# Layer 2 of the MLP recut as 448 columns per token block plus 128 turned ones, with the table magnitudes on GpSimd

## The chip, the cores and the metric

The kernel runs on one core of one Trainium2 chip. The metric is the device time of one launch in microseconds (us). An engine is called by its short name in the profile: PE is TensorE's matmul stream, PEld its weight loads, DVE VectorE, ACT ScalarE, POOL GpSimd, SP SyncE; a "q" behind a name is that engine's instruction queue (for DMAs: their issue).

## The reference

Input `u` has 2048 tokens of 576 channels. After a layer norm, two branches are computed and combined. One is a state-space convolution over time, done as an FFT over the tokens; the other is an MLP over the channels:

```python
x  = A_u
xn = layernorm(x)
s  = irfft(rfft(xn^T, 4096) * rfft(K, 4096))[:2048]^T + xn * D_skip   # K[d,t] = 2 Re sum_n C[d,n] exp(A[d,n] dt[d] t), n < 128
h  = gelu(layernorm(xn) @ w1 + b1)                                    # 576 -> 4608
g  = silu(h @ w2 + b2)                                                # 4608 -> 576
return x + s * g
```

All of it is float32. The change touches the second product, `h @ w2 + b2`, its accumulation, the final combination of its rows, and one step in making `K`.

## The kernel before

**The MLP.** Precision comes from splitting: each float32 operand is kept as a high and a low part in TensorE's faster float32 format, and each product is three matmuls (high·high, high·low, low·high). The hidden width 4608 is cut into 12 groups of G = 3 chunks of 128; the 2048 tokens into four blocks of 512, of which two (`tb` 0 and 1) are worked on in the first half of the program and two in the second. A **slot** is one group for one block of 512 tokens. There are 48 slots (numbered 0 to 47). In a slot, layer 1 (`layer1`, line 519) runs 14 matmuls of 512 columns for each of the three chunks. Behind each chunk stands a chain: ACT applies GELU from PSUM (line 552), ACT copies the high part `hh` (555), DVE subtracts for the low part `hl` (558). Layer 2 (`layer2`, line 585) then takes four token blocks `j` of 128: `hh`/`hl` of that block are the stationary operand (128x128) and `w2h`/`w2l` the moving one, in two halves of 288 columns. That makes 4 blocks x 3 chunks x 3 terms x 2 halves = 72 matmuls a slot. DVE adds the sum of each `j` from PSUM into `acc` in SBUF (595). `l2_terms` gives the order: the terms with chunks 0 and 1 of `j` 0 and a piece of `j` 1 come first, so that the chain of the third chunk has time.

**PSUM.** There are eight banks. The tile `cv` holds two pairs of banks for the convolution; `mxa` and `mxb` are one pair each and change roles every slot (`mx`).

**The convolution.** For each of 36 batches of 16 channels (NB), `tables` makes the values from which K is built: `load_par` (810, POOL's queue) fetches the parameters, DVE and ACT compute phases, cosines and sines, `mags` (853) multiplies out two tables of magnitudes `mg` (1024 and 512 elements a partition), and `weigh` (864 to 870) multiplies these with the cosines and sines into `U` and `v`. TensorE then runs `kgen` (910) and the FFT stages (982, 1021, 1074, 1106). This work stands between the MLP's matmuls on every engine.

**The order.** The class `Order` is a planner that runs when the program is built. It keeps a clock for each engine, adds an estimated duration for each step (`dve(n)`, `act(n)`, `pool(n)`, `L1`, `LEN`), and writes the instructions in the order of these clocks; the chip then executes each engine's instructions strictly in that order and the engines wait for each other by semaphores. Steps of the MLP are "urgent" and have due times (`hidden_by`, `add_by`); convolution steps fill in where they do not reach past a due time.

**The end.** The last slot accumulates on top of a seed: ACT copies `acc` into PSUM (`seed`, 567) ahead of the matmuls, ACT then applies SiLU from PSUM (678), DVE multiplies (687) and adds (697), and DMAs store the rows (700). In the slot before it, the rows of the other block are finished from SBUF (682, 689, 693, 697). `gate_store` stores the first half's gates to DRAM, where `combine` fetches them later. `FIRST` are the slots that start a sum (0, 3, 24, 25), `GATE` those that end one in the first half (20 and 23).

Of the kernel before, what the change touches and what calls it, by code (L numbers as in the profile page):

```python
# [38 lines left out]
TB = 512  # L39

# [172 lines left out]
def mixer_kernel(ctx, tc, u, log_a_real, a_imag, c_real, c_imag, log_dt, d_skip, w1, b1, w2, b2,  # L213
# [8 lines left out]
    def bank2(name):  # L222
        return ps.tile([P, 2, TB], F32, name=name, bufs=2 if name == "cv" else 1)
# [100 lines left out]
    acc = sb.tile([P, 8, D], F32, name="acc")  # L324

    def table_memory():

        t = [sb.tile([P, 2, SB, NV], F32, name="w", bufs=2) for _ in range(2)]  # L330
        t = [x.rearrange("p k c t -> p (k c t)") for x in t + [sb.tile([P, 2, SB, 64], F32, name="v")]]
        return [t[k // 3][:, k % 3 * D:(k % 3 + 1) * D] for k in range(8)]

    def x_load(b, queue=nc.sync, two=False):

        if b < 4:
            XT[b] = acc[:, 4 + b]
# [164 lines left out]
    HID, LAST, Q1, Q2 = {}, {}, {}, {}  # L502
    turn = [0]

    def mx(i):
        return "mxa" if (turn[0] + i) % 2 == 0 else "mxb"

    def layer1(g, tb, i):
        h, lo, r1, r2 = W[1]
        c = slice(i * P, (i + 1) * P)  # L510
        if i < 2:
            Q1[i] = bank2(mx(i))
        q = Q1[i % 2][:, i // 2]
# [7 lines left out]

    def first_layer1(i):
# [3 lines left out]
        if i != 1:  # L526
            Q1[i] = bank2("mxb" if i else "mxa")
        q = Q1[2][:, 0] if i == 2 else Q1[0][:, i]
        pairs = [(h, XH, 0), (h, XH, 1), (h, XL, 0), (h, XH, 2), (h, XL, 1), (h, XH, 3), (h, XL, 2), (h, XL, 3)]

        if i != 1:
            for j, (a, b, kb) in enumerate(pairs):
                for k in ((0, 1), (2,))[i // 2]:
                    nc.tensor.matmul(Q1[k // 2 * 2][:, k % 2], a[:, kb, k * P:(k + 1) * P], b[:, kb, 0],  # L534
                                     start=j == 0, stop=False)
        c = slice(i * P, (i + 1) * P)
        for kb in range(KB):
            nc.tensor.matmul(q, lo[:, kb, c], XH[:, kb, 0], start=False, stop=False)
        for r in (r1, r2):
            nc.tensor.matmul(q, r[:, c], XR[:, 0], start=False, stop=r is r2)  # L540

        return [hidden(0, 0, k, Q1[k // 2 * 2][:, k % 2]) for k in ((), (0, 1), (2,))[i]]
# [18 lines left out]
    def seed(tb, j, tile, halves=(0, 1)):  # L561

        d = slice(halves[0], halves[-1] + 1)
        q = bank2(tile)
        for dh in halves:
            SEED[j, dh] = q
        nc.scalar.activation(q[:, d, :288], acc[:, tb * 4 + j].rearrange("p (h d) -> p h d", h=2)[:, d], AF.Copy)

    SEED = {}

    def layer2(g, tb, j, terms, last, alone=False):
# [5 lines left out]
        c = slice(j * P, (j + 1) * P)  # L577
# [1087 lines left out]
```

## Time and profile before

| | |
|---|---|
| time, median of 3 runs | 1073.8 us (1073.32 to 1075.48) |
| the profiled execution's own time | 1074.78 us |
| its span | 1073.0 us |
| granted TensorE clock | 0.999 of full speed |
| first matmul of layer 1 | 12.89 us after the start |
| last matmul starts | 1067.41 us |
| largest group on PE | line 585, 3456 matmuls of 288 columns |
| largest group on DVE | line 558 (`hl`), 144 of 691 ns |
| largest group on POOL | line 810 (DMA issue), 36 of 764 ns |

The profile's page gives busy times of each engine, and the chain of work that ended last, followed back from the last instruction. Matmuls overlap in the pipeline and their ends are modelled, so the spacing of their starts, or the length of a merged piece of the chain divided by its number of matmuls, says more than the mean duration of one.

### The profile page before, as it was taken

The numbers are of one execution on the slowest core, as the hardware profiler recorded it, in microseconds if no ns is written. First come the engines' busy times: TensorE is split into PE (matmuls) and PEld (weight loads), VectorE is DVE, ScalarE is ACT, GpSimd is POOL, SyncE is SP. The second block draws the span as 40 slices with busy tenths as digits, with TensorE's granted clock in tenths as the row PEclk, the third lists the DMA queues.
The fourth block names the chain that finished last, engine by engine and source line by source line (L and its number), as shares of the span: only waits on it lengthen the run. The fifth ranks groups of instructions, "written<-read, shape, count | busy, mean of one in ns | idle before, by whom it ended". The sixth has DMA issues, their size and how long they took to land.

```text
span 1073.0 us, 25798 instructions
## 1 busy us (share of the span) xinstructions
PE 1065.7 (99%) x10703; PEld 926.8 (86%) x10703; DVE 952.1 (89%) x1530; ACT 693.3 (65%) x1063; POOL 206.8 (19%) x294
## 2 busy tenths in 40 slices
PE   9999999999999999999999999999999999999998
PEld 7989999888888888888888888788887888888887
DVE  7789968989898999999999989999999999866657
ACT  6656768867657586686866667667585676525353
POOL 6669433111000001100120000200011022322020
PEclk9999999999999999999999999999999999999999
DMA  7885455654223332356322233232431437454146
GB/s 230 240 257 194 130 194 197 209 116 130 74 66 106 50 90 73 108 142 145 89 73 77 68 75 97 50 99 64 87 97 43 132 100 167 123 185 135 38 117 168
DMA packets 139573, 129.62 MB, mean 121 GB/s; under 512 B 89628, under 2 KB 111296, under 8 KB 138432
## 3 DMA queue, kind: packets, MB, share of 16 engines
q1 hardware_dynamic: 122944, 78.31, 27.3%
q0 software_dynamic: 15760, 48.70, 15.0%
q8 instruction: 84, 1.38, 0.6%
q10 hardware_dynamic: 752, 0.97, 0.3%
q14 instruction: 33, 0.27, 0.1%
HBM read 98.50 MB, written 35.19 MB: 125 GB/s over the span
## 4 chain that ended last, share of the span: by engine, by line
PE 96%; DVE 2%; DMA 0%; ACT 0%; issue 0%; ACTq 0%; DVEq 0%
PE mxa L519 21%; PE mxb L585 21%; PE mxb L519 21%; PE mxa L585 21%; PE cv L910 3%; PE cv L1021 3%; PE cv L982 2%; PE cv L1074 2%; PE cv L1106 1%; DMA acc<-in_A_u_dram 0%; PE cv L585 0%; PE mxa L534 0%; DVE pr L749 0%; DVE row L394 0%; DVE acc L595 0%
## 5 line engine op out<-in xcount | busy, mean ns | idle before, releaser
L585 PE MATMUL mxb<-w2h,hh 128*128 128x288 f32 x573 | 170.2, 297 | 0.0
L585 PE MATMUL mxb<-w2h,hl 128*128 128x288 f32 x573 | 169.6, 296 | 0.0
L585 PE MATMUL mxb<-w2l,hh 128*128 128x288 f32 x573 | 168.6, 294 | 0.0
L585 PE MATMUL mxa<-w2h,hh 128*128 128x288 f32 x567 | 168.5, 297 | 0.0
L585 PE MATMUL mxa<-w2h,hl 128*128 128x288 f32 x567 | 167.9, 296 | 0.2 <-DVE hl L558 0.2
L585 PE MATMUL mxa<-w2l,hh 128*128 128x288 f32 x567 | 166.8, 294 | 0.0
L558 DVE TENSOR_TENSOR hl<-h,hh 128x512 fp32r<-128x512 f32 x144 | 99.3, 691 | 67.8 <-ACT hh L555 67.2
L810 POOL DMA_DIRECT2D par<-par_s x36 | 27.5, 764 | 463.9 <-DVE mg L853 412.2
L552 ACT ACTIVATE h<-mxa,b1t 128x512 f32<-128x512 f32 x73 | 50.1, 688 | 101.7 <-PE mxa L519 97.8
L585 PEld LDWEIGHTS mxb<-w2h,hh 128*128 128x128 f32 x573 | 107.6, 188 | 6.9 <-issue 3.0
L585 PEld LDWEIGHTS mxa<-w2h,hh 128*128 128x128 f32 x567 | 106.5, 188 | 7.4 <-issue 5.3
L585 PEld LDWEIGHTS mxb<-w2l,hh 128*128 128x128 f32 x573 | 107.6, 188 | 0.7
L585 PEld LDWEIGHTS mxb<-w2h,hl 128*128 128x128 f32 x573 | 107.5, 188 | 0.6 <-DVE hl L558 0.3
L585 PEld LDWEIGHTS mxa<-w2h,hl 128*128 128x128 f32 x567 | 106.4, 188 | 0.9 <-DVE hl L558 0.8
L585 PEld LDWEIGHTS mxa<-w2l,hh 128*128 128x128 f32 x567 | 106.5, 188 | 0.7
L552 ACT ACTIVATE h<-mxb,b1t 128x512 f32<-128x512 f32 x71 | 48.9, 689 | 74.8 <-PE mxb L519 71.1
L555 ACT ACTIVATE hh<-h 128x512 fp32r<-128x512 f32 x144 | 90.8, 632 | 4.1
L499 ACT ACTIVATE w2h<-raw 128x576 fp32r<-128x576 f32 x75 | 46.5, 675 | 56.5 <-PE mxa L585 53.5
L519 PE MATMUL mxa<-XH,w1h 128*128 128x512 f32 x284 | 78.7, 399 | 0.0
L519 PE MATMUL mxb<-XH,w1h 128*128 128x512 f32 x280 | 78.1, 401 | 0.0
L519 PE MATMUL mxa<-XL,w1h 128*128 128x512 f32 x284 | 76.2, 390 | 0.0
L519 PE MATMUL mxa<-XH,w1l 128*128 128x512 f32 x284 | 76.0, 389 | 0.0
(251 smaller groups left out, 2497.5 us busy)
## 6 DMA issues: line engine op xcount, KB each, us to landing
raw<-in_B_w_dram SPq DMA_DIRECT2D x75, 288.0 KB, 3.1
raw<-in_B_w_dram SPq DMA_DIRECT2D x100, 192.0 KB, 3.2
par_s<-A POOLq DMA_DIRECT2D x8, 1080.0 KB, 6.0
par<-par_s POOLq DMA_DIRECT2D x36, 240.0 KB, 3.3
f2t<-f2q SPq DMA_DIRECT2D x24, 256.0 KB, 3.3
raw<-in_B_w_dram SPq DMA_DIRECT2D x50, 96.0 KB, 3.6
u_s<-in_A_u_dram POOLq DMA_DIRECT2D x16, 288.0 KB, 4.5
xc<-xn_s SPq DMA_DIRECT2D x48, 96.0 KB, 3.7
```

Source lines behind the costliest of these rows:

```text
L499: nc.scalar.activation(h, r, AF.Copy)
L519: nc.tensor.matmul(q, a, b, start=j == 0, stop=j == len(ops) - 1)
L552: nc.scalar.activation(t, q, AF.Gelu_apprx_tanh, bias=b1t[:, g * G + i:g * G + i + 1], scale=1.0)
L555: LAST[0] = nc.scalar.activation(hh[:, i], t, AF.Copy)
L558: nc.vector.tensor_sub(hl[:, i], t, hh[:, i].bitcast(F32))
L585: nc.tensor.matmul(q[:, dh, :288], a[:, i, c], b[:, i, d], start=i == 0 and k == 0 and not alone, stop=i == G - 1 and k == 2, skip_group_c ...
L810: nc.gpsimd.dma_start(PAR[b].rearrange("p (g i) k -> p g (i k)", g=4), dram(par_s, (b // 6 * CH + b % 6 * 4) * NPAR, [[D * NPAR, P], [24 * ...
L910: nc.tensor.matmul(q[32 * g:32 * g + 32, i // 2, i % 2 * 64:i % 2 * 64 + 64], U[:, ri, 4 * g + i, :], v[:, ri, 4 * g + i, :], start=ri == ...
L982: nc.tensor.matmul(Q1ST[i, x][g // 2][64 * f:64 * f + 64, g % 2].rearrange(order), f1t[r].rearrange("p s k -> p (s k)"), rhs(r, f), start= ...
L1021: nc.tensor.matmul(Q[i][32 * q:32 * q + 32, f, 2 * ri:2 * ri + 2], m[r, 4 * i + q, 32 * ri:32 * ri + 32], A2[r, 4 * p + 2 * i + q // 2, :, ...
L1074: nc.tensor.matmul(QI[q // 2][64 * h:64 * h + 64, q % 2, i], MAT["g2t", p + h][r, i, ri], YS[p + h][0][r, i, ri], start=ri == 0, stop=ri == 1,
L1106: nc.tensor.matmul(Q[f][32 * e:32 * e + 32, t], g1t[r], A2[r, k:k + 2, 1].rearrange("p i d r -> p i r d"), start=True, stop=True, skip_gro ...
```

## The change

It has four parts.

1. **The recut.** Each token block `j` of layer 2 now takes 448 columns in one matmul per chunk and term: 36 matmuls of 448 columns a slot. The other 128 channels of all four token blocks are one piece with the key `"T"`: the stationary operand is `w2`'s 128 columns and the moving one `hh` or `hl` of all 512 tokens, so that the sum stands turned in PSUM (channels on partitions, 512 tokens along the bank): 9 matmuls of 512 columns. In four slots, `TURNED` = 20, 23, 46 and 47, the last ones of each token block, `"T"` is instead computed untransposed, as 36 matmuls of 128 columns. `acc` now holds 4 x 448 columns and 512 turned ones for each `tb`.
2. **Turning back.** Behind the last turned sum of each block (`CONV`: slots 18, 22, 44 and 45) DVE transposes 32x32 blocks into `bias2`, and 16 DMAs on SP put the blocks into place. Behind slot 22 `bias2` is loaded anew.
3. **PSUM and ACT.** `mxa` and `mxb` give way to four single banks `m0` to `m3`. Layer 1 uses banks 0, 1 and 2 for its chunks; layer 2 uses bank 3 for `j` 0, 0 for `j` 1, 1 for `"T"`, 2 for `j` 2 and again 3 for `j` 3. In 40 slots (`SEEDED`) ACT copies the turned sum from `acc` into bank 1 behind the second chunk's GELU, the matmuls add to it, and ACT copies it back out. In the other slots DVE does `"T"`'s addition.
4. **The magnitudes** (`mags`) move from DVE to POOL. The planner's constants and the rules for the last slot follow (there `j` 3 is cut into halves of 224 columns).

```diff
+DA = 448
+DT = D - DA
...
-        return ps.tile([P, 2, TB], F32, name=name, bufs=2 if name == "cv" else 1)
+        return ps.tile([P, 2, TB], F32, name=name, bufs=2)
+    def bank(k):
+        return ps.tile([P, TB], F32, name=f"m{k}")
...
+    def seed(tb, key):
+        q = SEED[key] = bank(BANK[key])
+        n = TB if key == "T" else DA
+        nc.scalar.activation(q[:, :n], rest(tb) if key == "T" else rows(tb, key), AF.Copy)
...
+        for j in range(4) if key == "T" and turned else (key,):
+            for i in terms:
+                for k, (a, b) in enumerate(((hh, h), (hh, lo), (hl, h))):
+                    kw = dict(start=i == 0 and k == 0 and not planted, stop=i == G - 1 and k == 2)
+                    if j == "T":
+                        a, b = ((hh, h), (hl, h), (hh, lo))[k]
+                        nc.tensor.matmul(q, b[:, i, DA:], a[:, i], skip_group_check=planted, **kw)
+                    elif key == "T":
+                        nc.tensor.matmul(q[:, j * DT:j * DT + DT], a[:, i, j * P:j * P + P], b[:, i, DA:],
+                                         skip_group_check=True, **kw)
+                    else:
+                        nc.tensor.matmul(q[:, c0:c1], a[:, i, j * P:j * P + P], b[:, i, c0:c1],
+                                         skip_group_check=alone, **kw)
...
+        def add():
+            if key != "T":
+                o = rows(tb, key)
+                nc.vector.tensor_add(o, q[:, :DA], bias2[:, :DA] if first else o)
+            elif first:
+                nc.vector.tensor_scalar(rest(tb), q, small[:, 6:7], None, op0=OP.add)
+            elif planted:
+                nc.scalar.activation(rest(tb), q, AF.Copy)
+            else:
+                nc.vector.tensor_add(rest(tb), q, rest(tb))
+    def turn_rest(tb):
+        nc.vector.transpose(bias2[:, :TB], rest(tb))
+    def place_rest(tb):
+        o = rest(tb).rearrange("p (j d) -> p j d", j=4)
+        x = bias2[:, :TB].rearrange("p (j v d) -> p j v d", j=4, v=4)
+        for c in range(4):
+            for v in range(4):
+                nc.sync.dma_start(o[32 * v:32 * v + 32, :, 32 * c:32 * c + 32], x[32 * c:32 * c + 32, :, v])
...
-            nc.vector.tensor_mul(T["m"][:, :, 64 * k:64 * k + 8 * n].rearrange("p c (i j) -> p c i j", i=n),
+            nc.gpsimd.tensor_mul(T["m"][:, :, 64 * k:64 * k + 8 * n].rearrange("p c (i j) -> p c i j", i=n),
...
-    LEN = [L1] * G + [3 * n * 0.1327 for n in (4, 2, 2, 4, 3, 3, 3, 3)]
+    MA, MT, MS, MH = 0.2, 0.2266, 0.075, 0.106
+    TURNED = (2 * NG - 4, 2 * NG - 1, 4 * NG - 2, 4 * NG - 1)
+    CONV = {2 * NG - 6: 0, 2 * NG - 2: 1, 4 * NG - 4: 0, 4 * NG - 3: 1}
+    BANK = {0: 3, 1: 0, 2: 2, 3: 3, "T": 1}
+    SEEDED = [k for k in range(4 * NG - 1) if k not in FIRST and k not in TURNED]
+    HEAD = [(0, allof[:-1], False), (1, allof[:-1], False), (0, allof[-1:], True), (1, allof[-1:], True)]
+    PLAN = {False: HEAD + [(2, allof, True), (3, allof, True), ("T", allof[:1], False), ("T", allof[1:], True)],
+            True: HEAD + [("T", allof, True), (2, allof, True), (3, allof[:1], False), (3, allof[1:], True)]}
...
-                [step("DVE", dve(2 * n), f(mags, 0), need=[("par", b)]),
-                 step("DVE", dve(n), f(mags, 1), mark=("mags", b))]
+                [step("POOL", pool(2 * n), f(mags, 0), need=[("par", b)]),
+                 step("POOL", pool(n), f(mags, 1), mark=("mags", b))]
...
-    ALONE = 7.0
+    ALONE = 5.0
```

What this does to the order of instructions is seen at three places. A row names the line, the operation, what is written <- what is read, and the shape written; the numbers behind a name tell buffers apart.

On PE, where layer 2 of an ordinary slot begins in the kernel before (a last layer 1 matmul into `mxa`, then `j` 0 into `mxb`):

```order
L519 MATMUL mxa_441<-XR_91,w1s_80 128x512
L585 MATMUL mxb_533<-w2h_459,hh_456 128x288
L585 MATMUL mxb_533<-w2l_460,hh_456 128x288
L585 MATMUL mxb_533<-w2h_459,hl_457 128x288
L585 MATMUL mxb_533<-w2h_459,hh_456 128x288
```

and where it ends in the changed kernel (the last three terms of `j` 3 in bank 3, then `"T"` in bank 1, chunk by chunk):

```order
L599 MATMUL m3_765<-w2h_628,hh_620 128x448
L599 MATMUL m3_765<-w2l_629,hh_620 128x448
L599 MATMUL m3_765<-w2h_628,hl_621 128x448
L594 MATMUL m1_706<-hh_620,w2h_628 128x512
L594 MATMUL m1_706<-hl_621,w2h_628 128x512
L594 MATMUL m1_706<-hh_620,w2l_629 128x512
```

A slot's layer 2 went from 72 of the first form to 36 of 448 columns and 9 of 512. In a slot of `TURNED`, here slot 20 behind the last terms of `j` 1 in bank 0, `"T"` is this form, 36 times, ahead of `j` 2:

```order
L599 MATMUL m0_4658<-w2h_4499,hh_4494 128x448
L599 MATMUL m0_4658<-w2l_4500,hh_4494 128x448
L599 MATMUL m0_4658<-w2h_4499,hl_4495 128x448
L596 MATMUL m1_4678<-w2h_4499,hh_4494 128x128
L596 MATMUL m1_4678<-w2l_4500,hh_4494 128x128
L596 MATMUL m1_4678<-w2h_4499,hl_4495 128x128
```

There the moving operand is down to 128 columns, with a new 128x128 stationary operand for each. On POOL, in the stretch where the parameters of the early batches are loaded, before:

```order
L299 DMA u_s<-in_A_u_dram 64x2x576 x2
L810 DMA par<-par_s 128x4x120
L299 DMA u_s<-in_A_u_dram 64x2x576 x2
L810 DMA par<-par_s 128x4x120 x5
L1117 DMA s_s<-pr 32x8x96 x4
L1117 DMA s_s<-ys 32x8x96 x4
```

and now, a little further on (line 880 is the load of parameters, 923 the magnitudes, 1187 the store of the convolution's result):

```order
L923 TENSOR_TENSOR mg<-par 128x16x64
L923 TENSOR_TENSOR mg<-par 128x16x32
L880 DMA par<-par_s 128x4x120
L1187 DMA s_s<-pr 32x8x96 x4
L1187 DMA s_s<-ys 32x8x96 x4
L923 TENSOR_TENSOR mg<-par 128x16x64
L923 TENSOR_TENSOR mg<-par 128x16x32
```

Two multiplications stand ahead of each load of parameters, and the stores of `s_s` stand between them. On SP, around the turning back of slots 44 and 45 (line 628), with the weight loads (473, 475, 478), the last parts of `s_s` (693) and the rows of `u` for the end (698):

```order
L475 DMA raw_92<-in_B_w1_dram 128x384 x4
L478 DMA raw_92<-in_B_w1_dram 64x384 x2
L628 DMA acc_87<-bias2_74 32x4x32 x16
L473 DMA raw_92<-in_B_w2_dram 128x576 x3
L628 DMA acc_87<-bias2_74 32x4x32 x16
L698 DMA A2_81<-u_s_65 128x576
L693 DMA w_10307<-s_s_64 128x96 x3
```

The 32 small DMAs are new; three loads of `w2` stand between the two sets, and the last reads of `s_s` and `u_s` stand behind the second.

More of the change, by code (lines that the diff above doesn't have):

```diff
@@ L559, in hidden @@
         return gelu, high, low
[L561 to L571, printed above, removed]
+    SEED, TT = {}, {}
+    def seed(tb, key):
+        q = SEED[key] = bank(BANK[key])
+        n = TB if key == "T" else DA
+        nc.scalar.activation(q[:, :n], rest(tb) if key == "T" else rows(tb, key), AF.Copy)
@@ L703, in finish @@
             st.append(step("DVE", dve(n), mul2))
[L704 removed]
+        return st + [step("DVE", dve(c2 - c0), total, need=[("x8", k)] + ([("rest", tb)] if c2 == D else []))]
     def params():
@@ L1354, in weigh_in @@
         m = KB + 1 if which == 1 else G
-        end = od.t["PE"] + sum(LEN[G:] if which == 1 else LEN[:G])
+        ln = lens(turn[0] - 1)
+        end = od.t["PE"] + sum(ln[G:] if which == 1 else ln[:G])
         for i in range(m):
```

246 lines of the change are left out of this document (148 added, 98 removed).

## The prediction

> **What bounds the kernel now.** I read the page first, then the table by stretches of 50 us, then the chain of work that ended last, and last the timelines of single slots and of the end.
>
> ```profile
> span 1073.0 us, 25798 instructions
> PE 1065.7 (99%) x10703; PEld 926.8 (86%) x10703; DVE 952.1 (89%) x1530; ACT 693.3 (65%) x1063; POOL 206.8 (19%) x294
> PE 96%; DVE 2%; DMA 0%; ACT 0%; issue 0%; ACTq 0%; DVEq 0%
> ```
>
> PE is busy for 99% of the span and holds 96% of the chain. A busy PE can hide gaps, so the second look is whether any stretch waits.
>
> ```profile
> 150.00:200.00 50.00, 50.00 (x351) 45.03 (x350) 42.33 (x63) 43.58 (x56) 11.05 (x20) 1.00 0.48 164
> ...
> 850.00:900.00 50.00, 50.00 (x538) 43.61 (x522) 49.16 (x81) 33.35 (x56) 9.62 (x17) 1.00 0.48 126
> ...
> 1050.00:1100.00 50.00, 17.70 (x108) 16.00 (x106) 15.81 (x24) 10.39 (x17) 0.00 (x0) 0.96 0.26 64
> ```
>
> The columns are PE, PEld, DVE, ACT and POOL, then the granted clock (1.00). PE fills each stretch from 150 to 1050, though DVE is at 49.16 of 50 in one of them. So the time is a start, PE's own work without a hole, and an end behind the last matmul; the change is worth what it takes from PE's work, unless it opens holes. The unit to count in is a slot's layer 2:
>
> ```profile
> 1032.37 3.44 PE mxa L519 x14
> 1035.81 3.17 PE mxb L519 x14
> 1038.98 1.58 PE mxa L585 x12
> 1040.56 0.79 PE mxb L585 x6
> 1041.35 0.79 PE mxa L585 x6
> 1042.14 1.60 PE mxb L585 x12
> 1043.74 2.38 PE mxa L585 x18
> 1046.12 2.38 PE mxb L585 x18
> ```
>
> Pieces of the chain, start and length. 72 matmuls of 288 columns take 1.58+0.79+0.79+1.60+2.38+2.38 = 9.52 us, 0.1322 each; 14 of 512 columns take 3.17, 0.2264 each. The 224 columns between cost 0.0942 us, 0.42 ns a column, and each matmul carries 0.011 us that doesn't depend on its columns. The gain sought lies in that 0.011.
>
> **The change, part by part.**
>
> *The recut, ordinary slots.* A matmul of 448 columns comes to 0.2264 - 64 x 0.00042 = 0.1995 us (between two measured sizes, so I trust it). A slot's layer 2 is then 36 x 0.1995 + 9 x 0.2264 = 7.18 + 2.04 = 9.22 us in place of 9.52: **-0.30 us**, in 44 slots **-13.2 us**. There are 45 weight loads in place of 72, none of them alone.
>
> *The four slots with untransposed rest.* They hold 36 matmuls of 128 columns, each with its own 128x128 weights. No row shows that form in the faster float32. Two kinds of row lie near.
>
> ```profile
> 11.71 0.27 PE L421 MATMUL mxb<-idp,row 128*128 128x128 f32 x1
> 11.82 0.60 PE L421 MATMUL cv<-idp,row 128*128 128x128 f32 x4
> 12.25 0.27 PE L421 MATMUL mxb<-idp,row 128*128 128x128 f32 x1
> L585 PEld LDWEIGHTS mxb<-w2h,hh 128*128 128x128 f32 x573 | 107.6, 188 | 6.9 <-issue 3.0 <-ACT w1h L499 1.2 <-DVE acc L595 0.6
> L910 PEld LDWEIGHTS cv<-v,U 128*32 128x32 f32 x2304 | 33.8, 110 | 9.6 <-issue 7.0 <-DVE mg L853 1.1 <-DVE hl L558 0.4
> ```
>
> The transposes at the start, 128x128 with 128 columns, begin 0.54 us / 5 = 0.108 us apart. And a load of 128 weight columns lasts 188 ns, one of 32 columns 110: 0.81 ns a column, so some 104 ns pass for 128 columns beside a fixed part that overlaps. A matmul of 128 columns by the line above streams in 0.065 us, so the load would be what paces it. Bounds: 0.065 from below (no matmul is quicker than its columns), 0.132 from above (the 288 form has the same load and more columns). I take 0.108, the nearest row in size. Then 36 x 0.108 = 3.89, with 7.18 for the rest 11.07 in place of 9.52: +1.55 a slot, **+6.2 us** for four (0 to +9.6 by the bounds). The last slot's halves of 224 columns, 18 at 0.108 instead of 9 at 0.1995, add **+0.15**. By the Trainium skill ("TensorE: Matmul & The Clock Gate", section "Back-to-back issue gap") a sustained pair of load and matmul at 128 columns takes about 81 ns; the sum would be 2.3 us in place of 6.2. No run here shows that form; the transposes' 0.108 speak for the slower value.
>
> *Transitions.* The number of convolution blocks between MLP matmuls is 76, before 74; the layer 1 piece behind one (1032.37, 3.44) is 0.27 longer than the next (3.17), so 2 x 0.27 = **+0.5 us**.
>
> *Seeds and copies on ACT.*
>
> ```profile
> L567 ACT ACTIVATE mxb<-acc 128x576 f32<-128x576 f32 x1 | 0.7, 657 | 0.0
> L555 ACT ACTIVATE hh<-h 128x512 fp32r<-128x512 f32 x144 | 90.8, 632 | 4.1
> ```
>
> A seed of 576 columns lasts 0.66 us, a copy of 512 0.63; 40 seeds and 40 copies come to some 80 x 0.63 = 50 us, ACT from 65% to 70%. What must be covered is the chain of the third chunk:
>
> ```profile
> 212.58 3.17 PE mxb L519 x14
> 215.75 1.03 PE cv L910 x64
> 215.79 0.69 ACT L552 ACTIVATE h<-mxb,b1t 128x512 f32<-128x512 f32 x1 [1.82 <-PE mxb L519]
> 216.51 0.63 ACT L555 ACTIVATE hh<-h 128x512 fp32r<-128x512 f32 x1
> 217.17 0.69 DVE L558 TENSOR_TENSOR hl<-h,hh 128x512 fp32r<-128x512 f32 x1 [1.57 <-ACT hh L555]
> ```
>
> From the end of layer 1 (215.75) to `hl` (217.86) pass 2.11 us. Here a convolution block (64 matmuls, 1.03 us) stands between; in a slot without one, PE reaches the third chunk after 12 + 6 matmuls, 2.38 us, before; after 12 of 448 columns, 2.39 us, now; `hl` is used two matmuls later. So the slack stays about 0.5 us. The seed stands behind the second chunk's GELU, with 3.17 us until the third one's: 0.69 + 0.63 + 0.66 fit. The copy out has layer 1's first chunk (3.17 us) before bank 1 is wanted. Cost **0**; where a table step stretches over it, a copy 0.6 us late would be a hole of that size.
>
> *The banks.*
>
> ```profile
> L595 DVE TENSOR_TENSOR acc<-mxa,acc 128x576 f32<-128x576 f32 x86 | 64.4, 748 | 11.0 <-PE mxa L585 10.8
> ```
>
> Bank 3 is used twice in a slot: `j` 3 needs `j` 0's addition done, and between lie 3 + 9 matmuls, 2.4 us. An addition of 576 columns lasts 0.75 us. Before, the same pair left 1.6 us (0.79 + half of 1.60). Cost 0.
>
> *Magnitudes on POOL.*
>
> ```profile
> L853 DVE TENSOR_TENSOR mg<-par 128x1024 f32<-128x1024 f32 x36 | 43.9, 1220 | 0.6
> L853 DVE TENSOR_TENSOR mg<-par 128x512 f32<-128x512 f32 x36 | 24.6, 684 | 0.0
> L496 POOL TENSOR_TENSOR w1l<-raw,w1h 128x384 fp32r<-128x384 f32 x2 | 2.0, 1014 | 0.0
> L810 POOL DMA_DIRECT2D par<-par_s x36 | 27.5, 764 | 463.9 <-DVE mg L853 412.2 <-issue 30.1 <-DVE kk L1037 21.6
> ```
>
> DVE loses 68.5 us of work. PE doesn't wait for DVE now, so this buys nothing directly, only slack. POOL needs 2.64 ns an element by its own row: 2.7 + 1.35 = 4.05 us a batch, 146 us in all, and has 866 us free. The multiplication needs only the parameters, as the phases do that DVE and ACT compute at the same time, and its result waits for the sines. POOL's queue already waited 412 us for DVE's magnitudes ahead of the next load. Cost 0, by that; whether POOL's reading slows DVE is the first rival.
>
> *Turning back, SP.*
>
> ```profile
> L1316 SPq DMA_DIRECT2D row<-y_s x36: 302/487/1534, 452.6 to 513.9; - x36
> L499 ACT ACTIVATE w2h<-raw 128x576 fp32r<-128x576 f32 x75 | 46.5, 675 | 56.5 <-PE mxa L585 53.5 <-DMA raw<-in_B_w_dram 1.7 <-PE mxb L585 1.3
> ```
>
> DMAs of like pieces take 0.49 us of issue (median): 16 make 8 us on SP. They start early in a slot whose `w2` loads come in its layer 2, so these leave up to a few us late; but ACT waits 53.5 us for PE before splitting `w2` and only 1.7 for its data, so the load has room. Cost 0; uncovered, up to 4 x 5 us.
>
> *The end.*
>
> ```profile
> 1067.41 0.29 PE L585 MATMUL mxb<-w2h,hl 128*128 128x288 f32 x1
> 1068.71 0.46 DVE L687 SCALAR_TENSOR_TENSOR v<-v,row 128x288 f32<-128x288 f32 x1 [0.25 <-ACT row L678]
> 1069.21 0.46 DVE L697 TENSOR_TENSOR A<-A,v 128x288 f32<-128x288 f32 x1
> ```
>
> Behind the last matmul (1067.5) DVE ends at 1069.67 and the stores at 1073.0: 5.5 us. In the changed order DVE has, after `"T"`, the sums of `j` 0 and 1 (0.75 each, as an addition of 576 columns), then `j` 2's pair (some 0.62 and 0.75) and two pairs of `j` 3 (0.35 to 0.5 each, below and about the 0.46 of 288 columns); counted from the end of `"T"`, 3.7 us ahead of the last matmul, they end about 2.2 us behind it, as now. Cost 0.
>
> **The sum.** -13.2 + 6.2 + 0.15 + 0.5 = -6.4 us on the profiled execution's 1074.8: 1068.4. That execution lies 1.0 above the median of the runs, 1073.8, so for a median **1067.5 us**.
>
> **The rivals.**
>
> *1. POOL's reads block DVE* (the slower side).
>
> ```profile
> 80.59 2.29 POOL L403 TENSOR_SCALAR w<-w,U 128x576 f32<-128x576 f32 x1
> 81.20 0.83 DVE L768 TENSOR_TENSOR A<-A,U 128x576 f32<-128x576 f32 x1
> 81.95 0.68 DVE L558 TENSOR_TENSOR hl<-h,hh 128x512 fp32r<-128x512 f32 x1
> ```
>
> Two DVE instructions with both inputs in SBUF begin inside a POOL one that reads SBUF, and `hl` keeps its usual 0.69; the other is 0.08 over an addition's 0.75. But POOL's form here has one tensor as input, the new one two. If the new form held DVE off, it would do so for 146 us in 72 pieces of 2.7 and 1.35 us, 14% of the time, for 1.1 us on average when hit (half a piece, weighted by length). `hl` of the third chunk, or an instruction queued ahead of it, is hit in 48 x 0.14 x 2 = 13 slots: 13 x 1.1 = 14 us where DVE's queue has used up the slack, 8 us where the slack of 0.5 is whole. In the middle +11: **1078.5**. It decides from a mean wait of 1 us per hit on; below 0.5 the slack covers it. The Trainium skill has this as a rule ("SBUF — State Buffer", section "Who interferes with whom"): a DVE instruction with two SBUF inputs and a POOL instruction that reads SBUF exclude each other, and the second waits until the first is done. By it the two DVE instructions above would have waited until 82.88; the trace does not agree for this POOL form.
>
> *2. The 128-column matmul streams freely* at 0.065 to 0.08 us: 36 x 0.07 = 2.5 instead of 3.89, -5.5 us in four slots: **1062**. For it: the fixed part of a load overlaps, and 64 loads of 32 columns pass in 1.0 us in the convolution. Against it: the 0.108 of the transposes.
>
> *3. The recut doesn't bring the 0.30:* holes of 0.3 us in each slot at bank 1 or bank 3, or a late seed, take it back in half the slots: 22 x 0.3 = 6.6, **1074**. For it: every slot has a new wait of PE on ACT. Against it: each has over 2 us of room.
>
> **How the numbers follow.** My sum holds with 0.57, rival 2 with 0.18, rival 3 with 0.12, rival 1 with 0.13. Range: down to 1060.6 (0.065 in all four slots), and up to 1075 to take in rival 3: 1060.5 to 1075, which leaves out rival 1 and little else. A measurement of this kernel can tell 0.2%, 2.1 us: faster means below 1071.7, slower above 1075.9. My sum with its own spread (1064 to 1071) and rival 2 are faster, 0.74; rival 3 and a little of rival 1 are the same, 0.15; the rest of rival 1 is slower, 0.11.
>
> **What would show it.** Right: layer 2 of an ordinary slot in the chain adds to 9.2 us; the 128-column matmuls start 0.108 apart; PE fills its stretches; POOL rises by 146 us and DVE falls by more than 68. Wrong: `hl` or the table products longer than 0.69 and 1.22 while POOL multiplies; PE or its loads waiting for ACT's copy or seed; matmuls of 448 columns wider apart than 0.20; weight splits waiting for DMA in the slots after 18, 22, 44 and 45.

## The result, and the profile after

| | before | after |
|---|---|---|
| time, median of 4 runs | 1073.6 us (1073.3 to 1075.5) | 1114.5 us (1113.0 to 1115.4) |
| ratio, 95% interval | | 1.038 (1.036 to 1.039) |
| span of the profiled execution | 1073.0 | 1111.9 |
| last matmul starts | 1067.4 | 1105.5 |

The kernel became slower by 41 us, where 6 us less were predicted. Nearly all of it lies ahead of the last matmul, so it is in PE's stream and not behind it. The page of the kernel after (span, busy times, chain by engine):

```profile
span 1111.9 us, 23735 instructions
PE 1076.8 (97%) x9524; PEld 881.5 (79%) x9524; DVE 938.0 (84%) x1469; ACT 724.7 (65%) x1134; POOL 355.5 (32%) x368
PE 64%; DVE 19%; issue 7%; ACT 4%; DMA 2%; POOL 2%; SPq 0%; ACTq 0%; DVEq 0%; POOLq 0%
```

POOL rose by 149 us, 144 of them the moved multiplications. But DVE, which lost 68.5 us of them, fell by only 14, and PE holds 64% of the chain in place of 96%: the end now runs through DVE again and again. What PE's matmuls waited for, in the kernel after (total, times, longest):

```profile
PE m L599 <- DVE hl L566: 12.6, 11, 3.5
PE m L599 <- DVE acc L609: 6.6, 5, 2.1
PE cv L1176 <- ACT hh L563: 6.5, 1, 6.5
```

Before, PE waited 0.2 us for `hl` and not at all for the other two. Two things are to be seen: many small waits for DVE, and one of 6.5 us that came once. A third thing comes with them. Behind a wait of 3.47 us for `hl`, the granted clock was 0.50 for 3.4 us, and matmuls of 448 columns, some 0.20 us apart elsewhere, started 0.37 apart (PE's timeline, then two stretches, whose granted clock is the third number from the end):

```profile
894.11 0.74 PE L599 MATMUL m<-w2h,hl 128*128 128x448 f32 x1 [3.47 <-DVE hl L566]
894.65 0.57 PE L599 MATMUL m<-w2h,hh 128*128 128x448 f32 x1
895.02 0.57 PE L599 MATMUL m<-w2l,hh 128*128 128x448 f32 x1
...
893.60:897.00 3.40, 2.89 (x8) 2.59 (x9) 2.07 (x4) 1.32 (x2) 3.26 (x6) 0.50 0.52 122
897.00:900.40 3.40, 3.40 (x40) 2.90 (x42) 1.61 (x3) 2.57 (x3) 0.21 (x1) 1.00 0.56 182
```

There are three such stretches ahead of the last matmul (from 487.4, 548.8 and 893.6, at or behind waits of 2.2, 6.5 and 3.5 us). PE works for 10 us in them, so some 5 us are lost by estimate; the kernel before has none there. Now the matmuls themselves, pieces of the chain after, an ordinary slot and then one with 128-column matmuls:

```profile
1052.65 7.29 PE m L599 x36
1059.94 2.07 PE m L594 x9
...
1073.30 3.64 PE m L599 x18
1076.93 3.97 PE m L596 x36
```

An ordinary slot's layer 2 takes 7.29 + 2.07 = 9.36 us, against 9.52 before: -0.16, in 44 slots -7.0. A slot with the untransposed rest takes 7.29 + 3.97 = 11.26: +1.74, in four +7.0. By these pieces the recut as such is worth nothing. Last, DVE's and POOL's instructions, grouped by form (busy, mean ns). The two products of DVE that make a batch's phases, before:

```profile
L828 DVE TENSOR_TENSOR w<-par,tv 128x1024 f32<-128x1024 f32 x36 | 43.8, 1216 | 1.9 <-DMA par<-par_s 1.9
L831 DVE TENSOR_TENSOR w<-w,par 128x512 f32<-128x512 f32 x36 | 24.7, 686 | 0.7
```

and these two (now lines 898 and 901), with `hl` and the larger of POOL's multiplications, after:

```profile
L566 DVE TENSOR_TENSOR hl<-h,hh 128x512 fp32r<-128x512 f32 x144 | 116.5, 810 | 76.6 <-ACT hh L563 76.3
L898 DVE TENSOR_TENSOR w<-par,tv 128x1024 f32<-128x1024 f32 x36 | 54.9, 1525 | 6.6 <-DMA par<-par_s 6.2
L901 DVE TENSOR_TENSOR w<-w,par 128x512 f32<-128x512 f32 x36 | 41.3, 1148 | 0.6
L923 POOL TENSOR_TENSOR mg<-par 128x1024 f32<-128x1024 f32 x36 | 89.7, 2492 | 399.5 <-DVE v L940 391.2 <-issue 8.3
```

`hl` took 691 ns before. The same instructions on the same data became longer. The timeline of DVE and POOL after, at one batch, shows how:

```profile
883.36 1.23 DVE L898 TENSOR_TENSOR w<-par,tv 128x1024 f32<-128x1024 f32 x1
883.41 4.50 POOL L923 TENSOR_TENSOR mg<-par 128x1024 f32<-128x1024 f32 x2 [19.15 <-DVE v L940]
884.62 2.35 DVE L901 TENSOR_TENSOR w<-w,par 128x512 f32<-128x512 f32 x1
886.90 1.57 DVE L566 TENSOR_TENSOR hl<-h,hh 128x512 fp32r<-128x512 f32 x1
```

POOL's two multiplications fill 883.41 to 887.91; the first of them ends at 886.42. The first DVE product was running already and keeps its 1.23. The next two last 2.35 and 1.57 in place of 0.69 each: one ends at 886.97, 0.55 behind the end of POOL's first, and `hl` at 888.47, 0.56 behind the end of its second. And POOL is let go by DVE's `v` (line 940, the last product of a batch): exactly where DVE goes on to the next batch's phase products.

### The profile page after: what moved, and what is told of

It reads as the page before. It is cut to its first block, busy times and chain, and to the rows that moved or that the text cites. A ratio compares the mean times of both kernels' runs of the same rounds, so it can differ in the third digit from the quotient of the medians.

```text
span 1111.9 us, 23735 instructions
## 1 busy us (share of the span) xinstructions
PE 1076.8 (97%) x9524; PEld 881.5 (79%) x9524; DVE 938.0 (84%) x1469; ACT 724.7 (65%) x1134; POOL 355.5 (32%) x368
## 3 DMA queue, kind: packets, MB, share of 16 engines
q8 instruction: 75, 1.23, 0.5%
## 4 chain that ended last, share of the span: by engine, by line
PE 64%; DVE 19%; issue 7%; ACT 4%; DMA 2%; POOL 2%; SPq 0%; ACTq 0%; DVEq 0%; POOLq 0%
PE m L528 27%; PE m L599 22%; PE m L594 6%; DVE w L898 2%; PE cv L1091 2%; DVE hl L566 2%; PE cv L980 2%; DVE w L901 2%; POOL mg L923 2%; PE m L596 1%; DVE A L1039 1%; DVE acc L609 1%; DVE w1l L510 1%; PE cv L1144 1%; DMA row<-y_s 1%
## 5 line engine op out<-in xcount | busy, mean ns | idle before, releaser
L923 POOL TENSOR_TENSOR mg<-par 128x1024 f32<-128x1024 f32 x72 | 143.7, 2011 | 399.6 <-DVE v L940 391.2
L599 PE MATMUL m<-w2h,hl 128*128 128x448 f32 x579 | 214.5, 370 | 12.8 <-DVE hl L566 12.6
L599 PE MATMUL m<-w2h,hh 128*128 128x448 f32 x579 | 215.8, 373 | 7.6 <-DVE acc L609 6.6
L599 PE MATMUL m<-w2l,hh 128*128 128x448 f32 x579 | 211.5, 365 | 0.0
L528 PE MATMUL m<-XH,w1h 128*128 128x512 f32 x564 | 156.4, 399 | 0.0
L528 PE MATMUL m<-XL,w1h 128*128 128x512 f32 x564 | 151.1, 390 | 0.0
L528 PE MATMUL m<-XH,w1l 128*128 128x512 f32 x564 | 150.8, 389 | 0.0
L599 PEld LDWEIGHTS m<-w2h,hl 128*128 128x128 f32 x579 | 109.4, 189 | 28.7 <-DVE hl L566 19.9
L599 PEld LDWEIGHTS m<-w2h,hh 128*128 128x128 f32 x579 | 109.3, 189 | 28.6 <-DVE acc L609 9.8
L599 PEld LDWEIGHTS m<-w2l,hh 128*128 128x128 f32 x579 | 109.4, 189 | 9.1
```

The lines of the kernel that those rows point to most:

```text
L528: nc.tensor.matmul(q, a, b, start=j == 0, stop=j == len(ops) - 1)
L599: nc.tensor.matmul(q[:, c0:c1], a[:, i, j * P:j * P + P], b[:, i, c0:c1], skip_group_check=alone, **kw)
L923: nc.gpsimd.tensor_mul(T["m"][:, :, 64 * k:64 * k + 8 * n].rearrange("p c (i j) -> p c i j", i=n), bc(PAR[b][:, :, e8:e8 + n], 3, 8), bc(P ...
```

## The experiments

Four theories were set against each other. A: POOL's multiplications, which read two tensors in SBUF, hold DVE's two-input instructions off, and PE waits behind DVE. B: ACT's seeds and copies in 40 slots, with their banks, open the holes. C: the turning back delays loads on SP's queue. D: the new order, which the planner writes, is what lost the time. All times are medians; the intervals of the ratios are about ±0.0017, or 1.8 us.

### One part at a time, planned anew

Magnitudes back on DVE, in the instruction and in the plan:

```diff
-            nc.gpsimd.tensor_mul(T["m"][:, :, 64 * k:64 * k + 8 * n].rearrange("p c (i j) -> p c i j", i=n),
+            nc.vector.tensor_mul(T["m"][:, :, 64 * k:64 * k + 8 * n].rearrange("p c (i j) -> p c i j", i=n),
...
-                [step("POOL", pool(2 * n), f(mags, 0), need=[("par", b)]),
-                 step("POOL", pool(n), f(mags, 1), mark=("mags", b))]
+                [step("DVE", dve(2 * n), f(mags, 0), need=[("par", b)]),
+                 step("DVE", dve(n), f(mags, 1), mark=("mags", b))]
```

> The changed kernel with the magnitudes back on VectorE (instruction and planned engine); the recut, the seeds and copies on ScalarE and the turned-back slots stay. Theory A (the two-input multiplications on GpSimd hold up VectorE instructions that read two SBUF inputs, and behind them hl and PE): the loss goes, PE is busy again for 98 to 99% of the span, about 1068 us (1064 to 1073), hl back to a mean of 0.69 us and the table products of 512 columns to 0.69 (with GpSimd's they were 0.81 and 1.15). Theory B (ScalarE's seeds and copies in 40 slots, or the three banks that go with them, open the holes): 1105 to 1115. Theory C (the turning back, whose 16 DMAs a time on SyncE's queue delay the loads behind them): 1105 to 1115.

Measured: 1091.2 us, ratio 1.016; `hl` 688 ns, line 901 686 ns. 23 us are gone, and the durations are back, but 17.5 us over the kernel before remain, more than theory A allowed.

The reverse of that diff, in the kernel before:

> The kernel before with one part of the change alone, the magnitudes on GpSimd (instruction and planned engine). Theory A: slower by most of what the changed kernel loses, 1100 to 1120 us, with hl at a mean of 0.8 us or more and maxima over 2 us, and PE under 98% busy. Theories B and C: 1072 to 1076, no change, since PE was the bound and VectorE only gains room.

Measured: 1107.6 us, ratio 1.031, `hl` 822 ns, PE at 97%, chain 65% PE and 21% DVE. Without any recut, seed or turning back, this one part costs 34 us. As A said.

The turned sums carried by DVE, without seeds:

```diff
-    SEEDED = [k for k in range(4 * NG - 1) if k not in FIRST and k not in TURNED]
+    SEEDED = []
```

> The changed kernel with no seeded slots: the 40 seeds and 40 copies of the turned sums on ScalarE go, and VectorE adds them up as it does the others (40 additions of 512 columns, some 27 us of VectorE work more); the magnitudes stay on GpSimd. Theory A: no better, 1110 to 1125, since the blocked VectorE gets more to do. Theory B: 1068 to 1075. Theory C: 1110 to 1115.

Measured: 1103.6 us, ratio 1.028, below the changed kernel, where A had no gain and B a much larger one. Both of these edits together:

> The recut alone: magnitudes on VectorE and no seeded slots. Theory A: 1066 to 1075, at or some us over the first of these four, since VectorE then has 27 us more than before (past 90% of the span) and no cover. Theory B: 1066 to 1070 and the first of the four over 1100. Theory C: 1105 to 1115.

Measured: 1114.8 us, ratio 1.038: no theory had it there beside 1091 for the first. So a new plan changes more than the part under test, and a comparison of two plans doesn't settle a part. The next runs keep the order of every engine.

### The order kept: what POOL reads

The changed kernel, where POOL only fills the tiles and the magnitudes are left out:

```diff
-            nc.gpsimd.tensor_mul(T["m"][:, :, 64 * k:64 * k + 8 * n].rearrange("p c (i j) -> p c i j", i=n),
-                                 bc(PAR[b][:, :, e8:e8 + n], 3, 8), bc(PAR[b][:, :, e1:e1 + 8], 2, n))
+            nc.gpsimd.memset(T["m"][:, :, 64 * k:64 * k + 8 * n].rearrange("p c (i j) -> p c i j", i=n),
+                                 1.0)
```

> The changed kernel, every engine's order kept, but GpSimd fills the 72 magnitude tiles with ones and reads nothing: the magnitudes are left out, the instructions on GpSimd stay. Theory A (GpSimd's two-input reads hold VectorE off): hl back to a mean of 0.69 us, the 512-column phase product from 1.15 to 0.69, the 37 us of holes in PE shrink to about 10, which are waits for DMA and ScalarE, 1078 to 1090 us. Theory D (the order and the queues of the changed plan make the holes, whatever GpSimd reads): 1105 to 1115.

And where it multiplies one tensor by a constant, and the other factor is left out:

```diff
+            nc.gpsimd.tensor_scalar(T["m"][:, :, 64 * k:64 * k + 8 * n].rearrange("p c (i j) -> p c i j", i=n),
+                                 bc(PAR[b][:, :, e1:e1 + 8], 2, n), 1.0, None, op0=OP.mult)
```

> The changed kernel, every engine's order kept, but GpSimd multiplies one tensor by a constant instead of two tensors: the other factor of the magnitudes is left out, the size and the place stay. Theory A as the trace of before had it (a one-input GpSimd instruction does not hold VectorE): hl near 0.69 us, 1078 to 1092. Theory A2 (any GpSimd instruction that reads SBUF holds VectorE): hl at 0.8 us, 1105 to 1118. Theory D: 1105 to 1115, hl at 0.8.

Measured: 1088.0 us (ratio 1.014) and 1098.9 (1.024), against 1114.5 with two inputs. The groups by form of the run that fills:

```profile
L566 DVE TENSOR_TENSOR hl<-h,hh 128x512 fp32r<-128x512 f32 x144 | 99.1, 689 | 109.0 <-ACT hh L563 108.0
L901 DVE TENSOR_TENSOR w<-w,par 128x512 f32<-128x512 f32 x36 | 24.7, 687 | 0.6
```

and of the run with one input:

```profile
L566 DVE TENSOR_TENSOR hl<-h,hh 128x512 fp32r<-128x512 f32 x144 | 105.5, 733 | 92.9 <-ACT hh L563 92.4
L901 DVE TENSOR_TENSOR w<-w,par 128x512 f32<-128x512 f32 x36 | 31.9, 885 | 0.6
L923 POOL TENSOR_SCALAR mg<-par 128x1024 f32<-128x1024 f32 x36 | 115.4, 3205 | 367.9 <-DVE v L940 362.1 <-issue 5.7
```

With nothing read DVE's instructions have their old lengths; with one tensor read they are longer, with two longest. In the three kernels DVE is busy for 877.7, 900.8 and 938.0 us with the same instructions: blocking costs it 23 and 60 us, and the time goes up by 11 and 26.5. It isn't POOL's own time: with one input POOL is busy longest (385 us, against 355.5). The timeline of the run with one input shows another kind of meeting:

```profile
224.23 3.79 POOL L923 TENSOR_SCALAR mg<-par 128x1024 f32<-128x1024 f32 x1 [15.38 <-DVE v L940]
225.42 1.41 DVE L901 TENSOR_TENSOR w<-w,par 128x512 f32<-128x512 f32 x1
```

Here the DVE product, twice its length, ends at 226.83, inside the POOL instruction, which lasts until 228.02 (3.79 us; the shortest of its kind took 2.76): both are slowed, neither waits for the other's end. The expectation had taken "one input" for free or as bad as two; it is between.

The kernel before in its own order, with the first diff's instruction alone moved (the plan still reckons with DVE):

> The kernel before in its own order on every engine, the planner still reckoning with VectorE, and only the 72 multiplications run on GpSimd. VectorE loses 68 us of work and nothing is moved. Theory A: hl at 0.8 us, PE with holes, 1090 to 1110. Theory D (a plan made anew is what lost the time in the run with the magnitudes alone): 1071 to 1076.

Measured: 1096.3 us, ratio 1.021, `hl` 821 ns, line 831 1096 ns. 22.7 us slower with 68.5 us of work taken from DVE and no other instruction moved: D can't explain this one. DVE was busy for 956.9 us, against 952.1 before, so the blocking took all of the relief here. And the other way round, the changed kernel in its order with the multiplications on DVE:

> The changed kernel with its whole order kept (the planner still reckons with GpSimd), only that the 72 multiplications run on VectorE, where they come in the program. VectorE has the 60 us that GpSimd's reads cost it in the changed kernel traded for 68.5 us of multiplications. Theory A (the relief of VectorE is given back by the blocking): about the same as the changed kernel, 1105 to 1118, with hl at 0.69 us. If the blocking costs more than its length, because it hits hl while PE waits for it: 1092 to 1104. If VectorE's load alone decides: 1115 to 1125.

Measured: 1098.5 us, ratio 1.022: 16 us less than the changed kernel, though DVE is as busy (934 us, against 938.0). Blocked time cost more here than work of the same length, as the second case of the expectation had it. The pair differs in a little more than that: with the multiplications gone from POOL's queue, DVE's wait for the parameters falls from 6.2 to 0.9 us, and there is one stretch at half clock in place of three. Against the run that fills, which has no multiplication at all, the same 72 cost some 10 us on DVE and 26.5 on POOL. So in this order DVE's load costs time even where nothing blocks it.

### The turning back on SP's queue

The filling run still has a hole in PE of 7.4 us, at 536. In the table of waits it stands as a wait for ACT's `hh`, but the chain behind that leads back over DVE's line 1406 to reads of `y_s`. SP and DVE ahead of it (in order of time):

```profile
506.77 10.80 SPq L628 DMA_DIRECT2D acc<-bias  x16
...
522.03 1.51 SPq L1401 DMA_DIRECT2D row<-y_s  x2
...
529.88 0.70 DVE L1406 STREAM_TRANSPOSE row<-row 64x512 f32<-64x512 f32 x1 [7.75 <-DMA row<-y_s]
```

16 DMAs take 10.8 us of issue, the bias reload and weight loads follow, then the last two reads of `y_s`, which the next block's layer 1 needs. So in the filling run that turning back (and its reload) goes to POOL's queue:

```diff
-    def place_rest(tb):
+    def place_rest(tb, queue=nc.sync):
...
-                nc.sync.dma_start(o[32 * v:32 * v + 32, :, 32 * c:32 * c + 32], x[32 * c:32 * c + 32, :, v])
+                queue.dma_start(o[32 * v:32 * v + 32, :, 32 * c:32 * c + 32], x[32 * c:32 * c + 32, :, v])
...
-                            place_rest(t2)
+                            place_rest(t2, nc.gpsimd if slot == 2 * NG - 2 else nc.sync)
                             if slot == 2 * NG - 2:
-                                nc.sync.dma_start(bias2[:, :DA], dram(b2, 0, [[0, P], [1, DA]]))
+                                nc.gpsimd.dma_start(bias2[:, :DA], dram(b2, 0, [[0, P], [1, DA]]))
```

> The kernel with the tiles filled by GpSimd (the magnitudes left out), and of the four turnings back the second one's 16 DMAs and the bias reload behind them issued by GpSimd instead of SyncE; all else in its place. Theory C2 (the hole of PE of 7.6 us at 536 comes from the last y_s reads, which stand on SyncE's queue behind these 16 DMAs of 0.6 us each): the hole shrinks to 1 us or less, 1080 to 1083. If the reads are late for another reason (the waits for the weights' tiles on the same queue): 1086 to 1089.

Measured: 1079.4 us, ratio 1.005, 8.5 less. SP and DVE in that run:

```profile
513.97 0.86 SPq L1401 DMA_DIRECT2D row<-y_s  x2
...
522.21 0.70 DVE L1406 STREAM_TRANSPOSE row<-row 64x512 f32<-64x512 f32 x1
```

The reads leave 8 us earlier and DVE no longer waits for them. PE waits 7.4 us less; the stretch of 6.8 us at half clock that began in the hole is gone too. The same edit in the changed kernel, and in the one with the multiplications on DVE:

> The changed kernel as it is, with the second turning back (16 DMAs and the bias reload) on GpSimd's queue. If the 8.5 us that this gave in the version without magnitudes is a cost of its own: 1104 to 1108. If the late reads of y_s are hidden there behind VectorE's blocked time, or GpSimd's queue, which also holds the magnitudes, brings a new wait: 1110 to 1118.

> The changed kernel in its order with both causes taken away at once: the magnitudes on VectorE, the second turning back on GpSimd's queue. If the two costs add: 16 and 8 us less than the changed kernel, 1088 to 1092. What then is left over the kernel before, some 15 us, is VectorE's load in this order (about 10, by the version without magnitudes) and the recut, which brings nothing. If something else costs time as well that was hidden: over 1094.

Measured: 1107.2 us (ratio 1.031), 7.4 less than the changed kernel, and 1089.4 (1.015), 25 less. The two costs add up, to within 2 us. PE's waits in the first of the two:

```profile
PE m L599 <- DVE hl L566: 12.5, 12, 3.5
PE m L599 <- DVE acc L609: 6.9, 6, 2.1
...
PE m L599 <- ACT hh L563: 0.9, 1, 0.9
```

The single wait of 6.5 us is gone, those for DVE stand as they were.

### The seeds

The filling run without the 40 seeds; the sums of the earlier slots are left out of `"T"`:

```diff
-        nc.scalar.activation(q[:, :n], rest(tb) if key == "T" else rows(tb, key), AF.Copy)
+        if turn[0] == NSLOT: nc.scalar.activation(q[:, :n], rest(tb) if key == "T" else rows(tb, key), AF.Copy)
...
-                kw = dict(start=i == 0 and k == 0 and not planted, stop=i == G - 1 and k == 2)
+                kw = dict(start=i == 0 and k == 0 and not alone, stop=i == G - 1 and k == 2)
```

> The kernel with the tiles filled by GpSimd, and without the 40 seeds of the turned sums on ScalarE (the sums of the earlier slots are left out of them; the 40 copies stay, the order is kept). By the prediction's step (seeds and copies cost nothing): 1086 to 1089. If seeds late behind other work of ScalarE make holes at bank 1 (rival 3 of the prediction): 1080 to 1085.

Measured: 1088.0 us, ratio 1.013, the same as with them. The prediction's zero for the seeds stands, and B falls as far as it was about them; the copies and the new banks weren't taken away.

### The plan

The kernel before with `ALONE = 5.0` in place of 7.0:

> The kernel before with one constant of its planner changed (ALONE 7 to 5, as the change has it), nothing else: the same instructions in another order. If the kernel before has an order that happens to be good, and any new plan loses some of it: 1077 to 1095, with waits of PE that the kernel before doesn't have. If the plan is robust: 1072 to 1076, and then what the recut versions lose must come from the recut itself.

Measured: 1076.2 us, ratio 1.0017 (1.0008 to 1.0026): 1.9 us from a whole new order. The kernel before isn't a lucky plan as far as this constant goes. Then the version with the magnitudes on DVE, with costs as measured:

```diff
-    MA, MT, MS, MH = 0.2, 0.2266, 0.075, 0.106
+    MA, MT, MS, MH = 0.2022, 0.2295, 0.1102, 0.1102
...
-    ALONE = 5.0
+    ALONE = 7.0
```

> The changed kernel with the magnitudes on VectorE and the planner's costs as measured: 0.2022 us for a matmul of 448 columns, 0.2295 for one of 512, 0.1102 for one of 128 (the plan had 0.075), and ALONE back from 5 to 7. If what is left in that version over the kernel before (17.5 us: 10 in holes of PE, 7 in an end that comes late on VectorE) is the plan's misjudged time: 1071 to 1082, with VectorE's end within 3 us of PE's. If it is the recut's own (banks, seeds, copies): 1086 to 1095.

Measured: 1103.2 us, ratio 1.028, outside both cases: 12 us worse, though PE's last matmul (1075.7) started 1.7 us earlier. The end moved away from PE. The last stores of the convolution's result in the kernel before:

```profile
1033.61 2.33 POOL L1117 DMA_DIRECT2D s_s<-pr  x4 [41.37 <-ACT pr L1114]
```

in this run:

```profile
1065.62 2.33 POOL L1187 DMA_DIRECT2D s_s<-pr  x4 [71.75 <-ACT pr L1184]
```

and in the recut alone:

```profile
1079.84 2.32 POOL L1187 DMA_DIRECT2D s_s<-pr  x4 [82.36 <-ACT pr L1184]
```

From these stores to the end of the span pass 34.9 us here (1100.5), 33.5 in the recut alone (1113.3), 32.8 in the first run (1057.6 to 1090.4): the rows' reads, products and stores hang on them. DVE's wait for the first of these reads, before and in this run:

```profile
1045.54 0.96 DVE L642 TENSOR_TENSOR xc<-xc,kt 128x768 f32<-128x768 f32 x1 [1.00 <-DMA xc<-s_s]
...
1078.75 0.96 DVE L676 TENSOR_TENSOR xc<-xc,kt 128x768 f32<-128x768 f32 x1 [13.40 <-DMA xc<-s_s]
```

If that path is as long in the kernel before, it could have ended there at about 1033.6 + 34 = 1068, 5 us ahead of the real end: by this estimate a second bound close behind PE. Three runs pace the convolution earlier:

```diff
-    END = 960.0
+    END = 930.0
```

> The changed kernel with the magnitudes on VectorE, planned anew with the convolution paced 30 us earlier (END 960 to 930). The same with END at 960 took 1091 us, with 7 us of it behind the last matmul, since the last stores of the convolution began at 1057.6 (before: 1033.6). If the late convolution is what is lost there: the stores begin by 1040 and the time is 1080 to 1086. If VectorE has no room for an earlier convolution: more holes in PE and 1088 to 1100.

> The same with the planner's costs as measured and ALONE 7. With END at 960 PE ended at 1075.7, and the stores of the convolution began at 1065.6, so that 23 us lay behind the last matmul. If only the pace was wrong: 1078 to 1085. If VectorE has no room: 1090 to 1105.

> The recut alone (magnitudes and turned sums on VectorE) with END 930. With END at 960: 1114.8 us, the stores of the convolution from 1079.8. If only the pace was wrong: 1080 to 1088. If VectorE's load (960 us busy) sets the end: 1095 to 1115.

Measured: 1088.4 us (ratio 1.013, stores at 1053.7), 1091.4 (1.016, at 1054.8) and 1103.0 (1.027, at 1067.2). The span follows the stores by 32.9, 34.2 and 33.7 us, so in all six of these versions the span ends with the convolution and not with PE (in the runs that keep the changed kernel's order, 46 to 47 us pass). The first time lies in the range of "more holes in PE", but PE waits no more there than with END at 960 (6.2 us in all, against 7.6). But 30 us of earlier pacing bring the stores only 4 to 13 us forward, and none comes near 1040: a constant doesn't mend it. What holds the convolution back, though in the first two of them DVE is busy for 938 to 940 us and was for 952 before, stays open.

## Why the prediction was wrong, step by step

The forecast was 1067.5 us; 47 us more were measured. By the runs:

| step of the prediction | predicted | measured | how |
|---|---|---|---|
| recut, 44 ordinary slots | -13.2 | -7.0 | pieces of the chain |
| four slots with 128 columns | +6.2 | +7.0 | pieces of the chain |
| magnitudes on POOL | 0 | +26.5 | same order, POOL reads nothing |
| turning back on SP | 0, at most 4 x 5 | +7.4 (8.5 in the filling run) | same order, other queue, one of four |
| seeds | 0 | 0 | same order, without them |
| the rest (transitions, halves, end) | +0.65 | about +5 | 3.3 in waits for `hl`, 1.1 in the end |

*The step that failed* is "Magnitudes on POOL", with its "Cost 0, by that". Its first half held: POOL had the room and nobody waits for the magnitudes. Its second, that POOL's reading wouldn't slow DVE, was left to rival 1 and argued there from two DVE instructions inside a one-input POOL instruction, one of them hardly longer and `hl` not at all. What the runs showed in its place: 60 us of blocked time on DVE and 26.5 us on the whole. Two instructions were too few, and the form was another one. Even the trace of before, some 20 us ahead of the lines that the prediction shows, had the sign:

```profile
58.73 2.29 POOL L403 TENSOR_SCALAR A<-A,U 128x576 f32<-128x576 f32 x1
59.17 0.93 DVE L558 TENSOR_TENSOR hl<-h,hh 128x512 fp32r<-128x512 f32 x1 [1.55 <-ACT hh L555]
...
61.98 2.29 POOL L403 TENSOR_SCALAR A<-A,U 128x576 f32<-128x576 f32 x1
62.34 1.01 DVE L558 TENSOR_TENSOR hl<-h,hh 128x512 fp32r<-128x512 f32 x1 [0.67 <-ACT hh L555]
```

Of the 11 `hl` that began inside such a POOL instruction there, three took 0.93 to 1.01 us and eight kept their length; the prediction read one of the eight. In the run with one input, 10 of 29 were longer.

It isn't the only step that failed. Without the magnitudes the kernel would still have taken 1088 us, 13 above the range: the turning back and the size of the recut were off as well, as told below.

*Rival 1 named the mechanism and its price was too low*, 11 us for 26.5, and with a chance of 0.13 it lay outside the range. It counted only `hl` of the third chunk and what stands ahead of it, hit at random in 14% of the time. But POOL isn't let go at random: line 940 releases it (391 of its 399.5 us of waiting), and the next things on DVE are lines 898 and 901 and often an `hl`, all with two inputs in SBUF. DVE lost 17 us in `hl`, 28 in the two phase products, 11 in `w2l` (895 ns, before 753). So of the 68.5 us of relief 60 came back, as stalls in front of the instructions that PE waits for. That this was worse than the same work on DVE, the pair of runs in one order shows: 1114.5 against 1098.5. Of the 26.5 us against the filling run, PE's waits make 17, and the matmuls at half clock some 3 by estimate; the rest isn't assigned.

*POOL's time* came out right in part by luck: 145 us for the forecast 146. The shortest of its multiplications took 1.96 and 1.07 us, so undisturbed ones would make about 36 x 3.03 = 109 us by estimate. The row from which the forecast took its price per element was for another shape, and the rest is POOL's own lengthening where it meets DVE (the eight multiplications that met no such DVE instruction took 1.96 to 1.97 and 1.07 to 1.10 us).

The Trainium skill has the rule of rival 1 ("SBUF — State Buffer", section "Who interferes with whom"): a DVE instruction with two SBUF inputs and a GpSimd instruction that reads SBUF shut each other out, and whoever comes second waits; one that only writes doesn't disturb. The trace agrees for two inputs (2.35 and 1.57 us for 0.69) and for the filling (0.69). For POOL's one-input form it doesn't: the product that ended at 226.83 would have had to wait for POOL's end at 228.02.

*The recut's size.* The mechanism, fewer and longer matmuls, was right; the size was read off a line between 288 and 512 columns of two different layers. 448 columns take 7.29/36 = 0.2025 us in place of 0.1995, and `"T"` 2.07/9 = 0.230 in place of 0.2264. Three ns in each of 45 matmuls are 0.14 us of the 0.30 a slot. Why layer 2's long matmuls start wider apart than layer 1's wasn't tried. The 128-column form took 3.97/36 = 0.110, as the transposes' 0.108 had said and not 0.065 to 0.081; rival 2 is out.

*Turning back.* Its issue was put at 8 us and at no cost, as the weight splits have room. They had. Late were the reads of `y_s`, which the prediction hadn't named though they stand on the same queue (it took their 0.49 us as the price of a DMA; these took 0.60 to 0.68). Only one of the four turnings back was tried on another queue; its 7.4 to 8.5 us lie above the bound of 5 us for one.

*Seeds, copies, transitions, end.* The zero for the seeds is shown; the copies weren't taken away. Behind the last matmul's start lie 6.4 us after and 5.6 before.

*The rest.* With neither magnitudes nor late reads the kernel stands 5.1 us over the one before (1079.4 against 1074.3 in the same series), though the recut's terms cancel; PE there waits 3.5 us for `hl`, before 0.2, and 6.7 us lie behind the last matmul's start, before 5.6. With the magnitudes on DVE, 15.7 us remain in the kept order and 14 to 41 in new ones. In the new ones the convolution's end is late; a cause beyond that isn't shown.

## What to carry to other kernels

Before moving an elementwise step from DVE to POOL, list what DVE does at that moment: if those instructions read two tensors in SBUF, expect that POOL's reading takes from DVE much of what the move gave (here 60 of 68.5 us), and where others wait. Look at every meeting of the two engines that the trace has, not at one. An engine that is released by another starts in step with it, so a hit rate from shares of the span is no estimate. Where a planner writes the order, compare parts in a kept order, and look for the path that ends just ahead of the present bound: here, by that estimate, 5 us were all that PE could have gained before the convolution's end took over.

## What the runs showed of the hardware

- A POOL multiplication of two SBUF tensors and a DVE instruction with two SBUF inputs hold each other off: two DVE instructions in a row ended 0.55 and 0.56 us after the ends of POOL's two, and took 2.35 and 1.57 us for 0.69. An addition with one input in PSUM isn't held: the 12 of line 609 that met such a multiplication took 0.58 to 0.62 us, as all others.
- A one-input POOL instruction slows some of such DVE instructions without stopping them: 0.69 became 1.41 us. A fill on POOL, 0.96 us for 1024 elements, doesn't touch them: the 17 `hl` that met one took 0.65 to 0.69 us.
- 16 small DMAs took 10.8 us of SP's queue, 0.68 each; without them, the reads behind left 8 us earlier.
- At or behind three waits of PE of 2.2 to 6.5 us the granted clock was 0.50 for 3.4 to 6.8 us, and matmuls of 448 columns started 0.37 us apart in place of 0.20.
- Matmuls of 128 columns with their own 128 weight columns started 0.110 us apart, no closer than those of 224 (0.111).
